# Reordering the opening of a GFNet-plus-FFN kernel: all x at once, five weight buffers, weight conversions in other places

## The chip, the cores and the metric

The kernel runs on one core of a Trainium2 chip. The metric is device time in microseconds (us) of one execution; with one core there is no slowest core to choose.

Engines are named as in the profile: PE is TensorE's matmuls, PEld its weight loads, DVE is VectorE, ACT is ScalarE, POOL is GpSimd, SP is SyncE. L312 is line 312 of the kernel in question; the changed kernel's lines differ by one or so from those of the kernel before, past the first helpers.

## The reference

```python
batch, seq, dim = (8, 3008, 256);  n_tokens, d_model, d_ff = (24064, 256, 2048)

def _attn_ref(x, filt_r, filt_i):
    X = np.fft.rfft(x, axis=1)
    F = (filt_r + 1j * filt_i)[None, :, :]
    return np.fft.irfft(X * F, n=x.shape[1], axis=1).astype(np.float32)

def _moe_ref(x, w_in, w_out):
    h = x @ w_in
    g = np.where(h > 0.0, h, np.exp(np.minimum(h, 0.0)) - 1.0)
    return (g @ w_out).astype(np.float32)
# out = _moe_ref(_attn_ref(x, filt_r, filt_i).reshape(B * S, D), w_in, w_out)
```

A filter along the sequence is followed by a two-layer network of width 2048 over all tokens. The weights arrive as 64-bit numbers and are turned into 32-bit ones on the core.

## The kernel before

The Fourier transform of length 3008 is done as two factors (47 and 64), with an intermediate z written to HBM and read back in another order. The second factor multiplies by the filter and goes part of the way back; its result goes through HBM again (yd) and is read per block of tokens. Then comes the token loop: 8 batches of 6 blocks, four *quads* each, a quad being one quarter of the hidden width for one block, some 13.6 us long. From batch 1 on, the transform of the next batch is hidden in the token loop. For batch 0 there is nothing to hide it behind: that is the opening, and the change is only about it.

```python
def x_load(b, c, queue=nc.sync):                  # one of six chunks of x, 4 buffers
    t = xs[b, c] = xp.tile([P, XC, D], FP32, tag="xc", name="xc")
    ...
    w = tas[b, c] = tap.tile([P, XC, P], FP32, tag="ta", name="ta")
    queue.dma_start(w, ta_d[:, ts(c, XC), :])
    ...

def a_unit(b, c):                                 # first factor, one chunk
    t = t1s[b, c] = t1p.tile([P, XC, D], FP32, tag="t1", name="t1")
    for r in (0, 2):
        ...matmuls into psa
        nc.scalar.activation(out=t[:, r:r + 2, :], in_=ps, func=AXT.Copy)

def b_unit(b, g, f=None):                         # second factor, one of eight units
    ...matmuls of t (a read of z) into psr ("re"), psi ("im")
    nc.vector.tensor_tensor(out=sr, in0=re, in1=f[:, 0], op=ALU.mult)
    nc.vector.tensor_tensor(out=si, in0=re, in1=f[:, 1], op=ALU.mult)
    nc.vector.tensor_tensor(out=p, in0=im, in1=f[:, 1], op=ALU.mult)
    nc.vector.tensor_tensor(out=q, in0=im, in1=f[:, 0], op=ALU.mult)
    nc.gpsimd.tensor_tensor(out=sr, in0=sr, in1=p, op=ALU.subtract)
    nc.gpsimd.tensor_tensor(out=si, in0=si, in1=q, op=ALU.add)

def bi_unit(b, g):                                # the way back
    ...matmuls into pa ("pva"), pb ("pvb")
    nc.scalar.activation(out=t[:, 0:2, :], in_=pa, func=AXT.Copy)
    nc.scalar.activation(out=t[:, 2:4, :], in_=pb, func=AXT.Copy)

def w_convert(k):                                 # piece k of 16, 512 KB of 64-bit numbers
    nc.vector.tensor_scalar(out=m, in0=hi, ...)                        # wm, the mask
    nc.scalar.activation(out=l, in_=lo, func=AXT.Identity, ...)        # wl
    nc.scalar.activation(out=f, in_=m, func=AXT.Identity, ...)         # wf: waits for wm
    ...four operations on e, one on f, one product, all on VectorE
    if j % 2 == 1:                                                     # odd pieces only
        ...four VectorE sums of the seven-product scheme
```

Pieces 4q and 4q+1 belong to the first layer's quarter q, 4q+2 and 4q+3 to the second layer's. In the traces of this case VectorE and ScalarE run their instructions in the program's order (below, a ScalarE copy that stands behind conversion 10 starts only at 121.10, behind that conversion's step at 120.08), so the place of a `w_convert` sets what stands behind it on both. The order of the opening before:

```python
for k in range(2):
    w_fetch(k)                                    # GpSimd's queue, 3 buffers
for c in range(XBUFS):                            # 4
    x_load(0, c, nc.scalar)
...
w_fetch(2)
f_read_first(ff)                                  # the filter, 3.1 MB, GpSimd's queue
for c in range(NXC):                              # 6
    a_unit(0, c)
    if c + XBUFS < NXC:
        x_load(0, c + XBUFS, nc.scalar)
    z_write(0, c)
    w_convert(c)
    w_fetch(3 + c)
z_read(0, 0)
z_read(0, 1)
for g in range(NG + 2):                           # 8 units, bi_unit two behind b_unit
    ...bi_unit(0, g - 2), b_unit(0, g, ff[:, g]), z_read(0, g + 2), y_write(0, g - 2)
    if g % 2 == 1:
        k = 6 + g // 2
        w_convert(k)
        w_fetch(k + 3)
...
y_read(0, 0)
w_convert(11)
w_fetch(14)
...
n_unit(0, 0)                                      # first matmuls on tokens ("psn")
x_load(1, 0)
...
for k in range(12, 16):                           # behind quads 0, 0, 1, 2
    at((0, 0, 1, 2)[k - 12], 1, w_convert, k)
```

## Time and profile before

| | before |
|---|---|
| time, 3 runs | 2762.31 us median (2762.2 to 2765.57) |
| span of the profiled run, granted clock | 2761.7 us, 0.980 |
| first VectorE multiplication of the second factor ("S") | 74.79 us |
| first matmul on tokens | 131.14 us |
| first matmul of quad 1 | 153.31 us |

The prediction below shows the page and the stages. More lines of the timeline; columns are start, length, engine, line, operation, output<-inputs, and in brackets the idle time of the engine ahead of it and what ended it:

```profile
120.30 0.59 ACT L239 ACTIVATE t<-pvb 128x512 f32<-128x512 f32 x1
...
131.14 3.75 PE L266 MATMUL psn<-tn,t 128*128 128x128 f32 x16 [11.41 <-DMA t<-yd]
...
133.79 0.39 DVE L288 TENSOR_TENSOR ys<-y 128x224 f32<-128x224 f32 x1 [2.10 <-ACT y L268]
```

The last copy of the second factor ends at 120.89, the array starts on tokens when the read of yd has landed, and the first VectorE operation on tokens waits for ScalarE's copy, so VectorE has time to spare there. The second factor itself, from S to the start of conversion 9, in the view by stretch (stretch, length, busy time of PE, PEld, DVE, ACT, POOL, granted clock, DMA share, GB/s):

```profile
74.79:115.49 40.70, 28.10 (x115) 8.92 (x108) 36.53 (x58) 9.78 (x18) 21.12 (x20) 0.63 0.57 156
```

and the waits of its VectorE for the array, over the 44 us from 0.8 us behind S (instruction, releaser, us in total, times, longest):

```profile
DVE sr L223 <- PE psi L211: 3.2, 2, 2.1
```

VectorE is busy 36.53 of 40.70 us there and waits only 3.2 us for the array.

### The profile page before, as it was taken

The numbers are of one execution on the slowest core, as the hardware profiler recorded it, in microseconds if no ns is written. First come the engines' busy times: TensorE is split into PE (matmuls) and PEld (weight loads), VectorE is DVE, ScalarE is ACT, GpSimd is POOL, SyncE is SP. The second block draws the span as 40 slices with busy tenths as digits, with TensorE's granted clock in tenths as the row PEclk, the third lists the DMA queues.
The fourth block names the chain that finished last, engine by engine and source line by source line (L and its number), as shares of the span: only waits on it lengthen the run. The fifth ranks groups of instructions, "written<-read, shape, count | busy, mean of one in ns | idle before, by whom it ended". The sixth has DMA issues, their size and how long they took to land.

```text
span 2761.7 us, 36465 instructions
## 1 busy us (share of the span) xinstructions
PE 2661.4 (96%) x13376; PEld 2281.0 (83%) x13376; DVE 2021.7 (73%) x3428; ACT 1331.3 (48%) x2281; POOL 268.4 (10%) x322
## 2 busy tenths in 40 slices
PE   2689999999999999999999999999999999999998
PEld 1288778987899878998789877898789987899887
DVE  4777877777776777767776787767877677777776
ACT  2254455544455444554455544454454544454544
POOL 3311210002000120001200021000210012000000
PEclk7599999999999999999999999999999999999999
DMA  9654421433114331242313332143321223110100
GB/s 227 174 136 119 106 56 30 115 90 99 43 47 117 76 91 37 70 115 71 79 50 87 87 88 68 37 106 94 97 61 39 72 69 94 37 39 19 25 22 16
DMA packets 141634, 214.51 MB, mean 78 GB/s; under 512 B 25268, under 2 KB 99142, under 8 KB 141456
## 3 DMA queue, kind: packets, MB, share of 16 engines
q1 hardware_dynamic: 122656, 173.60, 24.7%
q0 software_dynamic: 17792, 36.93, 5.4%
q8 instruction: 106, 1.74, 0.3%
q10 hardware_dynamic: 1008, 1.64, 0.2%
q14 instruction: 72, 0.59, 0.1%
HBM read 137.04 MB, written 78.12 MB: 78 GB/s over the span
## 4 chain that ended last, share of the span: by engine, by line
PE 86%; DVE 7%; ACT 3%; DMA 2%; issue 2%; POOL 0%; SPq 0%; DVEq 0%; ACTq 0%; POOLq 0%
PE po L385 37%; PE pha L312 11%; PE phc L312 11%; PE phd L312 11%; PE phb L312 5%; PE psa L167 3%; PE psn L266 2%; PE pva L211 2%; PE psr L211 2%; PE pso L424 2%; DVE g L317 1%; ACT e L323 1%; ACT e L324 1%; DVE c L403 1%; DVE g L328 1%
## 5 line engine op out<-in xcount | busy, mean ns | idle before, releaser
L385 PE MATMUL po<-g,wo 128*128 128x256 f32 (+1 forms) x5376 | 1324.2, 375 | 0.0
L385 PEld LDWEIGHTS po<-g,wo 128*128 128x128 f32 x5376 | 1021.5, 190 | 116.2
L323 ACT ACTIVATE e<-g 128x512 f32<-128x512 f32 (+1 forms) x576 | 357.6, 621 | 599.5 <-DVE g L317 599.3
L324 ACT ACTIVATE e<-e 128x512 f32<-128x512 f32 (+1 forms) x768 | 477.6, 622 | 24.4
L312 PE MATMUL pha<-y,wi 128*128 128x256 f32 (+1 forms) x1536 | 396.3, 380 | 8.7 <-ACT g L332 8.6
L317 DVE TENSOR_TENSOR g<-phc,g 128x512 f32<-128x512 f32 (+1 forms) x384 | 259.5, 676 | 194.9 <-PE phc L312 194.8
L328 DVE SCALAR_TENSOR_TENSOR g<-e,g 128x512 f32<-128x512 f32 (+1 forms) x576 | 387.4, 673 | 11.6 <-ACT e L324 11.1
L323 ACT ACTIVATE e<-pha 128x512 f32<-128x512 f32 (+1 forms) x192 | 113.0, 588 | 531.1 <-PE pha L312 531.1
L312 PEld LDWEIGHTS pha<-y,wi 128*128 128x128 f32 x1536 | 285.2, 190 | 93.1 <-ACT t L238 34.1
L317 DVE TENSOR_TENSOR g<-phd,g 128x512 f32<-128x512 f32 (+1 forms) x384 | 261.0, 680 | 87.0 <-PE phd L312 66.0
L328 DVE SCALAR_TENSOR_TENSOR g<-e,pha 128x512 f32<-128x512 f32 (+1 forms) x192 | 129.4, 674 | 257.8 <-ACT e L324 257.8
L227 POOL TENSOR_TENSOR sr<-sr,sp 128x512 f32<-128x512 f32 x64 | 81.1, 1268 | 1304.4 <-DVE sp L225 1304.4
L312 PE MATMUL phc<-ys,wi 128*128 128x256 f32 (+1 forms) x768 | 195.5, 377 | 2.6 <-DVE si L224 2.6
L312 PE MATMUL phd<-y,wi 128*128 128x256 f32 (+1 forms) x768 | 195.4, 377 | 1.3
L312 PE MATMUL phb<-ys,wi 128*128 128x256 f32 (+1 forms) x768 | 193.8, 375 | 0.4 <-DVE ys L290 0.4
L312 PE MATMUL phc<-y,wi 128*128 128x256 f32 (+1 forms) x768 | 194.0, 375 | 0.0
L312 PE MATMUL phd<-ys,wi 128*128 128x256 f32 (+1 forms) x768 | 193.7, 375 | 0.0
L312 PEld LDWEIGHTS phc<-ys,wi 128*128 128x128 f32 x768 | 145.3, 191 | 23.7 <-issue 7.8
L312 PEld LDWEIGHTS phd<-y,wi 128*128 128x128 f32 x768 | 145.3, 191 | 22.5 <-PE phc L312 6.5
L332 ACT ACTIVATE g<-pha 128x512 f32<-128x512 f32 (+1 forms) x192 | 112.7, 587 | 105.3 <-PE pha L312 105.1
L312 PEld LDWEIGHTS phb<-ys,wi 128*128 128x128 f32 x768 | 145.8, 190 | 17.2 <-PE pha L312 0.7
L312 PEld LDWEIGHTS phd<-ys,wi 128*128 128x128 f32 x768 | 145.8, 190 | 16.5
(98 smaller groups left out, 2781.1 us busy)
## 6 DMA issues: line engine op xcount, KB each, us to landing
z<-t SPq DMA_DIRECT2D x192, 128.0 KB, 3.8
t<-z SPq DMA_DIRECT2D x128, 192.0 KB, 3.7
yd<-t SPq DMA_DIRECT2D x128, 192.0 KB, 2.8
t<-yd SPq DMA_DIRECT2D x192, 128.0 KB, 4.1
xc<-in_x_dram SPq DMA_DIRECT2D x88, 256.0 KB, 4.6
out_dram<-o SPq DMA_DIRECT2D x176, 128.0 KB, 2.4
f<-fd POOLq DMA_DIRECT2D x112, 192.0 KB, 3.6
tn<-tn_t SPq DMA_DIRECT2D x48, 256.0 KB, 4.2
```

What stands on the lines that cost most here:

```text
L167: nc.tensor.matmul(ps[:, u, :], w[:, r + u, :], xt[:, r + u, :], start=True, stop=True)
L211: nc.tensor.matmul(ps[:, u:u + w, :], table[k, v, :], rhs[k, u:u + w, :], start=True, stop=True)
L227: nc.gpsimd.tensor_tensor(out=sr, in0=sr, in1=p, op=ALU.subtract)
L266: nc.tensor.matmul(ps[:, ts(q, P)], t[:, i - 4 * m, ds(dh * P, P)], w[:, i - 4 * m, :], start=True, stop=True)
L312: nc.tensor.matmul(banks[key][:, a, 0:h], w_in[q][:, COMBO[n], a, :], y[n], start=start and a == 0, stop=True, skip_group_check=True)
L317: nc.vector.tensor_tensor(out=g[o], in0=i0, in1=i1, op=ALU.add)
L323: nc.scalar.activation(out=e, in_=src, func=AXT.Relu, scale=-1.0)
L324: nc.scalar.activation(out=e, in_=e, func=AXT.Exp, scale=-1.0)
L328: nc.vector.scalar_tensor_tensor(out=g[n], in0=es[n], scalar=1.0, in1=src, op0=ALU.subtract, op1=ALU.max)
L332: nc.scalar.activation(out=g["t1"], in_=mm(1, "a", True), func=AXT.Copy)
L385: nc.tensor.matmul(po[i][:, u, 0:h], w_out[q][:, COMBO[n], a, :], g[n][:, a, :], start=q == 0 and a == 0 and n in (1, 3, 6, 4), stop=True, ...
L424: nc.tensor.transpose(ps[0:w, u, ts(dh, P)], c[dh][:, ds((2 * a + u) * P, w)], eye)
```

## The change

The intent: let the first factor go at the pace of x, with nothing of the weights ahead of its copies; keep the transfers full by loading weights further ahead; take the next batch's x out of the stretch in which the first tokens' data are read back; and take the last weight pieces out of it too. `wait_x(c)` and the copy into `junk` below are one-element copies on GpSimd that wait until a load has landed, and so hold back the loads that stand behind them in GpSimd's order. Besides, the filter is read in two halves and its buffer is cleared on GpSimd instead of VectorE.

```diff
-            zs[b] = zp.tile([96, K2, D], FP32, tag="z", name="z")
+            zs[b] = zp.tile([96, K2 + 1, D], FP32, tag="z", name="z")
 ...
-        wd = wds[k] = fbufs[k % FBUFS]...
+        wd = wds[k] = wbufs[k % 5 if k < 12 else (2, 0, 1, 2)[k - 12]]...
 ...
+        CONVERTS = {1: 6, 3: 7, 5: 8, 7: 9, 8: 10, 9: 11}
+            wbufs += [... "wb%d" ... for i in range(2)]
+            more = [(... "xb%d", ... "tb%d") for i in range(NXC - XBUFS)]
             for k in range(2):
                 w_fetch(k)
-            for c in range(XBUFS):
-                x_load(0, c, nc.scalar)
-            nc.vector.memset(ff, 0.0)
+            for c in range(NXC):
+                x_load(0, c, nc.scalar, more[c - XBUFS] if c >= XBUFS else None)
+            nc.gpsimd.memset(ff, 0.0)
 ...
+            w_convert(0)
+            w_convert(1)
+            wait_x(3)
             w_fetch(2)
-            f_read_first(ff)
+            w_fetch(3)
+            wait_x(5)
+            for a in range(2):
+                f_read_first(ff, a)
+            for k in range(4, 7):
+                w_fetch(k)
             for c in range(NXC):
                 a_unit(0, c)
-                if c + XBUFS < NXC:
-                    x_load(0, c + XBUFS, nc.scalar)
                 z_write(0, c)
-                w_convert(c)
-                w_fetch(3 + c)
+            for k in range(2, 6):
+                w_convert(k)
+                w_fetch(k + 5)
 ...
-                if g % 2 == 1:
-                    k = 6 + g // 2
-                    w_convert(k)
-                    w_fetch(k + 3)
+                if g in CONVERTS:
+                    w_convert(CONVERTS[g])
+                if g == 1:
+                    w_fetch(11)
+                if g == 4:
+                    w_fetch(12)
+                if g in (5, 6):
+                    x_load(1, g - 5)
 ...
-        w_convert(11)
-        w_fetch(14)
+        w_convert(12)
+        nc.gpsimd.tensor_copy(out=junk[0:1], in_=t4s[0, 0][0:1, 0, 0:1])   # the read has landed
+        for k in (13, 14, 15):
+            w_fetch(k)
         n_unit(0, 0)
-        x_load(1, 0)
 ...
-        for k in range(12, 16):
-            at((0, 0, 1, 2)[k - 12], 1, w_convert, k)
+        for k in (13, 14, 15):
+            at(max(k - 14, 0), 1, w_convert, k)
```

More of the change, by code (lines that the diff above doesn't have):

```diff
@@ L145, in raw, with x_load @@
         return bass.AP(tensor=src.tensor, offset=src.offset + row * D, ap=ap)
-    def x_load(b, c, queue=nc.sync):
-        t = xs[b, c] = xp.tile([P, XC, D], FP32, tag="xc", name="xc")
+    def x_load(b, c, queue=nc.sync, place=None):
+        t, w = place or (xp.tile([P, XC, D], FP32, tag="xc", name="xc"), tap.tile([P, XC, P], FP32, tag="ta", name="ta"))
+        xs[b, c], tas[b, c] = t, w
         skip = 1 if c == 0 else 0
@@ L153, in x_load @@
             nc.gpsimd.memset(t[64:P, 0, :], 0.0)
-        w = tas[b, c] = tap.tile([P, XC, P], FP32, tag="ta", name="ta")
         queue.dma_start(w, ta_d[:, ts(c, XC), :])
@@ L178, in z_write @@
             r0 = p * H + c * XC
-            nc.sync.dma_start(zs[b][r0:r0 + XC, :, :].rearrange("n k d -> k n d"), t[p * 32:p * 32 + 32, :, :])
+            nc.sync.dma_start(zs[b][r0:r0 + XC, 0:K2, :].rearrange("n k d -> k n d"), t[p * 32:p * 32 + 32, :, :])
     def z_read(b, g):
@@ L189, in f_read, with f_read_first @@
             nc.gpsimd.dma_start(t[r].rearrange("p c u d -> p (c u d)"), fd[g, a].rearrange("q c u d -> q (c u d)"))
-    def f_read_first(t):
+    def f_read_first(t, a):
+        r = a * 64
         for c, src in enumerate((filt_r, filt_i)):
-            for a in range(2):
-                r = a * 64
-                nc.gpsimd.dma_start(t[r:r + 24, :, c, :, :].rearrange("q g u d -> q g (u d)"),
-                                    raw(src, 2 * a, [[64 * D, 24], [4 * D, NG], [1, 2 * D]]))
-                for u in range(2):
-                    g0 = 1 if a == u == 0 else 0
-                    for r0, n in ((24, 16), (40, 7)):
-                        nc.gpsimd.dma_start(t[r + r0:r + r0 + n, g0:NG, c, u, :],
-                                            raw(src, 64 * (r0 - 23) - 4 * g0 - 2 * a - u,
-                                                [[64 * D, n], [-4 * D, NG - g0], [1, D]]))
-            nc.gpsimd.dma_start(t[24:48, 0, c, 0, :], raw(src, 32, [[64 * D, 24], [1, D]]))
+            nc.gpsimd.dma_start(t[r:r + 24, :, c, :, :].rearrange("q g u d -> q g (u d)"),
+                                raw(src, 2 * a, [[64 * D, 24], [4 * D, NG], [1, 2 * D]]))
+            for u in range(2):
+                g0 = 1 if a == u == 0 else 0
+                for r0, n in ((24, 16), (40, 7)):
+                    nc.gpsimd.dma_start(t[r + r0:r + r0 + n, g0:NG, c, u, :],
+                                        raw(src, 64 * (r0 - 23) - 4 * g0 - 2 * a - u,
+                                            [[64 * D, n], [-4 * D, NG - g0], [1, D]]))
+            if a == 0:
+                nc.gpsimd.dma_start(t[24:48, 0, c, 0, :], raw(src, 32, [[64 * D, 24], [1, D]]))
     def tile_mm(ps, table, k, rhs, special):
@@ L440 @@
     wds = {}
+    wbufs = list(fbufs)
     def w_fetch(k):
         q, j = divmod(k, 4)
-        wd = wds[k] = fbufs[k % FBUFS].bitcast(U32).rearrange("p c u d -> p (c u d)").rearrange("p (a w) -> p a w", w=2)
+        wd = wds[k] = wbufs[k % 5 if k < 12 else (2, 0, 1, 2)[k - 12]].bitcast(U32).rearrange("p c u d -> p (c u d)").rearrange("p (a w) -> p a w", w=2)
         if j < 2:
@@ L513, with wait_x @@
     with tc.manual_schedule():
+        CONVERTS = {1: 6, 3: 7, 5: 8, 7: 9, 8: 10, 9: 11}
         with tc.tile_pool(name="boot", bufs=1) as bp:
             ff = bp.tile([P, NG, 2, 2, D], FP32, name="ff")
+            wbufs += [bp.tile([P, 2, 2, D], FP32, name="wb%d" % i) for i in range(2)]
+            more = [(bp.tile([P, XC, D], FP32, name="xb%d" % i), bp.tile([P, XC, P], FP32, name="tb%d" % i))
+                    for i in range(NXC - XBUFS)]
+            def wait_x(c):
+                nc.gpsimd.tensor_copy(out=junk[0:1], in_=xs[0, c][0:1, 0, 0:1])
             for k in range(2):
                 w_fetch(k)
-            for c in range(XBUFS):
-                x_load(0, c, nc.scalar)
-            nc.vector.memset(ff, 0.0)
-            nc.gpsimd.tensor_copy(out=junk[0:1], in_=xs[0, 2][0:1, 0, 0:1])
+            for c in range(NXC):
+                x_load(0, c, nc.scalar, more[c - XBUFS] if c >= XBUFS else None)
+            nc.gpsimd.memset(ff, 0.0)
             for t, d in ((gb, gb_d), (gr, gr_d), (gi, gi_d)):
                 nc.gpsimd.dma_start(t, d)
+            w_convert(0)
+            w_convert(1)
+            wait_x(3)
             w_fetch(2)
-            f_read_first(ff)
+            w_fetch(3)
[4 more added lines that the diff above has]
+                w_fetch(k)
             for c in range(NXC):
                 a_unit(0, c)
-                if c + XBUFS < NXC:
-                    x_load(0, c + XBUFS, nc.scalar)
                 z_write(0, c)
-                w_convert(c)
-                w_fetch(3 + c)
+            for k in range(2, 6):
+                w_convert(k)
+                w_fetch(k + 5)
             z_read(0, 0)
@@ L567, in at @@
             plan.setdefault((quad, place), []).append((fn, a))
-        for c in range(1, XBUFS):
-            at(c - 1, 0, x_load, 1, c)
-        for k in range(12, 16):
-            at((0, 0, 1, 2)[k - 12], 1, w_convert, k)
-        at(0, 1, w_fetch, 15)
+        for c in range(2, XBUFS):
+            at(c - 2, 0, x_load, 1, c)
+        for k in (13, 14, 15):
+            at(max(k - 14, 0), 1, w_convert, k)
         at(3, 1, f_arrange)
```

## The prediction

> **What bounds the kernel now.** I began with the page: share of busy time, then the row of slices.
>
> ```profile
> PE 2661.4 (96%) x13376; PEld 2281.0 (83%) x13376; DVE 2021.7 (73%) x3428; ACT 1331.3 (48%) x2281; POOL 268.4 (10%) x322
> ...
> PE   2689999999999999999999999999999999999998
> ...
> PEclk7599999999999999999999999999999999999999
> DMA  9654421433114331242313332143321223110100
> ```
>
> TensorE is busy except in the first two slices (69 us each), and these are also the only ones with a low granted clock and the ones with the busiest DMA. Next I asked for busy time by stretch. From 300 to 2700 us TensorE works 2396.10 of 2400 us, so nothing there is to be had from waits; the change leaves that part's instructions alone. Everything is decided before quad 1 of the token loop (a quad is one quarter of the hidden width for one block of tokens) settles at about 153 us:
>
> ```profile
> 0.00:30.00 30.00, 12.43 (x40) 8.48 (x40) 17.80 (x24) 8.00 (x13) 9.64 (x21) 0.99 1.00 241
> 30.00:75.00 45.00, 7.91 (x25) 4.78 (x28) 15.53 (x33) 7.48 (x13) 12.97 (x23) 0.50 0.88 208
> 75.00:121.00 46.00, 32.12 (x123) 9.57 (x116) 41.66 (x64) 12.58 (x24) 23.88 (x22) 0.61 0.54 146
> 121.00:131.00 10.00, 0.00 (x0) 0.00 (x0) 9.55 (x21) 2.38 (x4) 1.91 (x4) 0.50 0.89 265
> 131.00:153.00 22.00, 14.59 (x68) 13.36 (x68) 14.46 (x30) 9.65 (x18) 1.24 (x2) 0.81 1.01 245
> ```
>
> The columns are the stretch, its length, busy time of PE, PEld, DVE, ACT, POOL, clock, DMA share, GB/s. Four stages follow. First factor, 0 to 75: DMA is full and no engine is. Second factor, 75 to 121: VectorE is busy 41.66 of 46 us. Then 10 us in which TensorE waits for the result through HBM. Then the first quad and a hole. The chain of waits, in order of time, says which transfers the first stage hangs on:
>
> ```profile
> 4.40 11.32 DMA xc<-in_x_dram
> ...
> 20.04 13.04 DMA ff<-in_filt_r_dram
> 33.90 11.16 DMA ff<-in_filt_i_dram
> ...
> 47.58 6.99 DMA f<-in_moe_w_out_dram
> ...
> 63.43 4.87 DMA z<-t
> 68.36 4.28 DMA t<-z
> ```
>
> First x, then the filter, then a weight piece queued behind it, then the conversion of that piece on ScalarE and VectorE, and only behind it in ScalarE's order the copies of the last two x chunks, whose write to z comes last. The timeline gives the start of the second factor, and the hole of the last stage:
>
> ```profile
> 74.79 0.69 DVE L223 TENSOR_TENSOR sr<-psr,ff 128x512 f32<-128x512 f32 x1 [5.65 <-PE psi L211]
> ...
> 122.60 0.42 DVE L470 TENSOR_SCALAR wm<-f 128x512 uint32<-128x512 uint32 x1
> ...
> 153.31 1.86 PE L312 MATMUL pha<-y,wi 128*128 128x224 f32 x4 [7.05 <-ACT g L332]
> ```
>
> **What the Trainium skill says.** "DMA: Bandwidth & Descriptors", section "Issuing engines are not separate DMA queues": transfers of all issuing engines run on the same 16 DMA engines and interleave. The trace agrees: between 30 and 40 us the SyncE queue took 59.1% and the GpSimd queue 46.8%, together only 201 GB/s. So reordering moves waits, but does not make bytes cheaper. The same page, section "Latency and other measured facts", tells of loss at large power-of-two HBM row pitches, smallest 512 KiB; here z goes from a 32 KiB pitch to 33 KiB, which that table does not reach. "SBUF — State Buffer", section "Who interferes with whom": a VectorE tensor_scalar that enters a two-port mode and a GpSimd operation exclude each other. The trace agrees: L474 takes 0.42 us alone, 1.49 us beside GpSimd's 1.45 us addition. "TensorE: Matmul & The Clock Gate", section "What's actually happening": after an idle window the array runs at half clock. The trace agrees: after the 7.05 us hole four matmuls took 1.86 us instead of 0.92.
>
> **Part by part.** I call S the first VectorE multiplication of the second factor (74.79 before) and reckon the rest from it.
>
> *First stage.* Removed: the wait of x chunk 5 for a buffer (landed at 41), and the ScalarE copies standing behind conversions that wait for weights. So z no longer hangs on weights and should be complete near 50 instead of 68. But conversions 2 to 5 now all stand in VectorE's order after the x copies and ahead of the first multiplication, and pieces 4 and 5 are queued behind the filter. So S hangs on piece 5. Bytes until then: x 3.1 MB, its tables 1.6, z 3.1, filter 3.1, six pieces of 0.52 = 3.1, second-factor tables 0.2, two reads of z 0.8: 15.0 MB. At before's rates, 241 GB/s to 30 us (7.2 MB) and 218 GB/s from 30 to 68 (the DMA view of that stretch), the other 7.8 MB take 36 us: piece 5 at 66. With fewer stalls of the queues, as between 60 and 70 (234 GB/s), 63. Behind it: a conversion without sums took VectorE 3.7 us in before (122.60 to 126.25), one with its four sums 5.5 (54.66 to 60.12); conversions 4 and 5 in a row, from piece 4's landing some 2 us earlier (0.52 MB at 234 GB/s), end 5.5 to 7 us behind piece 5. S = 68.5 to 73, I take **70: 4.8 us won**. Pieces 6 and 7, which before moved in this stage, move later.
>
> *Second factor.* Eight units with four multiplications of 0.6 us each and a conversion after every second stay as they were, with VectorE as the limit. But the new place of conversions (after units 1, 3, 5, 7, then two in the tail) puts conversion 10 ahead of the last unit's two ScalarE copies. In before these copies ran at 119.81 to 120.90. Now they follow ScalarE's second step of conversion 10, which waits for VectorE's mask, at 122.60 in before, because conversion 9 with its sums is ahead. Mask 0.42, ScalarE 0.63, copies 1.1: end at 124.8 in before's time. **3.9 us lost.**
>
> *Through HBM.* Before, from the last copy to the first matmul was 131.14 less 120.90 = 10.2 us: 3.8 for the write, 1.3 issue, 5.0 for the last read, beside weights and the next x at 265 GB/s. x now goes during the second factor, where DMA was 54% busy, and weights 13 to 15 wait until the read has landed. A read of this kind takes 2.4 us when alone (80 to 125 us); so write 3.0, issue 1.3, read 3.0: 7.3. **2.9 won.** But VectorE now has conversions 9 to 12 in a row, 7.1 + 3.7 + 5.4 + 3.7 = 19.9 us from 115.47, to 135.4 in before's time; the tokens' first subtraction, 133.79 before, stands behind: it comes at +1.6. So of 3.9 - 2.9 = +1.0, +1.5 remains.
>
> *First quads.* The hole stays: two conversions still stand after quad 0, ahead of the copy L332 of quad 1. They were 12 and 13 (sums last), now 13 and 14: 13's four sums stand before 14's mask, so the copy comes 4 x 0.43 = 1.7 us later: **+1.7**. Conversion 15 moves one quad earlier and leaves the quad after it: TensorE lost 1.6 us there between 181 and 195; I count -0.5.
>
> Sum: -4.8 + 1.5 + 1.7 - 0.5 = -2.1 us. I go somewhat lower, to **2757**, because the bytes' rate is the softest term and a queue that never stalls, or the padded z, would raise it: 15.0 MB at 260 GB/s would give piece 5 at 60 and S at 65.
>
> **Rivals.** (1) *z is the bound and weights are not*: if S followed z (50 + read 4.5 + units' matmuls 2) S would be 58 and the time 2748. For it: in before VectorE waited 5.65 us for the psi matmuls, behind z. Against: the order of instructions puts conversion 5 first. (2) *The filter's transfers bound*: in before it took from 18.6 to about 53 us to issue and land. Now it starts once the last x has landed, about 30; the same 34 us would make it 64, and pieces 4 and 5 land at 67 to 69; S = 74, nothing won, and +2.7 from the rest: 2765. (3) *Padding z does much*: all reads and writes of z faster. In the loop that would be hidden (TensorE 99.8% busy); in the opening worth perhaps 3 us. (4) *A fuller second factor*: x of 1.5 MB among the reads of z could delay a unit; DMA is half idle there, so I give it at most 1 us.
>
> **Range and chances.** The first stage can lie from 0 to 14 us better, the rest +1 to +5 worse: 2748 to 2764 for eight in ten. Two per cent is 55 us, over a third of the whole opening, so same is nearly certain.
>
> **What the new profile would show.** z complete near 50 and its reads waiting no more for ScalarE; the first L223-like multiplication at 68 to 72, released by a conversion rather than by matmuls; the last pair of copies of the second factor behind a conversion's ScalarE step; last read of yd in about 3 us; and a hole of 8 to 9 us before quad 1. Wrong it would be if the multiplication started before 64 or after 75, if the hole were gone, or if the loop after 300 us had changed its pace.

## The result, and the profile after

| | before | after |
|---|---|---|
| time, 4 runs each of the same rounds | 2763.66 us (2762.2 to 2765.57) | 2762.14 us (2761.47 to 2763.48) |
| span of the profiled run | 2761.7 us | 2761.7 us |
| ratio | | 0.9995, 95% interval 0.9977 to 1.0012 |

Ratios, here and below, are the mean time of one kernel's runs over that of the other's of the same rounds, so not quite the ratio of the medians quoted. The change does nothing that can be measured, and the prediction's range and class hold; its point was 5 us too low. The profile says that a lot moved nonetheless, though not in the slices of the page, where the row of granted clocks still shows two low slices:

```profile
PEclk7599999999999999999999999999999999999999
```

The stages after, in the view by stretch:

```profile
0.00:30.00 30.00, 14.78 (x43) 10.06 (x44) 11.84 (x22) 8.34 (x13) 16.96 (x24) 1.00 1.00 267
30.00:69.00 39.00, 6.49 (x19) 3.15 (x18) 16.11 (x34) 7.72 (x13) 13.93 (x25) 0.54 1.06 224
69.00:122.00 53.00, 37.25 (x124) 9.77 (x122) 46.16 (x74) 13.61 (x25) 22.70 (x20) 0.53 0.60 162
122.00:130.00 8.00, 0.27 (x1) 0.30 (x2) 7.66 (x17) 2.60 (x4) 2.05 (x4) 0.50 0.82 217
130.00:154.00 24.00, 15.12 (x69) 13.57 (x68) 18.17 (x36) 9.89 (x18) 1.06 (x2) 0.78 0.70 199
```

Against the stretches of before: the first stage is 6 us shorter, at 267 and 224 GB/s instead of 241 and 208. The second is 7 us *longer* (53 instead of 46). The wait for the first tokens' data is 2 us shorter, and the first quad with its hole (the idle time of TensorE ahead of quad 1) 2 us longer (24 instead of 22), with VectorE busy 18.17 us there instead of 14.46.

The chain of waits of the first stage after, in order of time (start, length, what):

```profile
13.37 7.94 DMA xc<-in_x_dram
21.33 7.04 DMA z<-t
28.38 14.76 DMA z<-t
...
45.69 13.17 DMA z<-t
58.91 7.77 DMA t<-z
...
66.82 0.65 PE psi L211
```

The filter and the weights have left this chain. What took their place is z itself: three writes of it took 7.0, 14.8 and 13.2 us, and the last part of the read that the first unit needs was issued only at 58.91. The timeline shows that the other chain ends at the same moment:

```profile
59.83 0.43 DVE L471 TENSOR_SCALAR wm<-wb 128x512 uint32<-128x512 uint32 x1 [7.61 <-DMA wb<-in_moe_w_in_dram]
...
68.51 0.42 DVE L494 TENSOR_TENSOR wi<-wi 128x256 f32<-128x256 f32 x1
68.89 0.69 DVE L223 TENSOR_TENSOR sr<-psr,ff 128x512 f32<-128x512 f32 x1
```

Piece 4 lands at 59.83, conversions 4 and 5 run back to back for 9.06 us, and the first multiplication follows at 68.89 without a gap. The array's psi for it is done at about 68.8, too.

Now the end of the second factor and the start of the tokens:

```profile
119.63 0.42 DVE L471 TENSOR_SCALAR wm<-f 128x512 uint32<-128x512 uint32 x1
120.08 0.63 ACT L473 ACTIVATE wf<-wm 128x512 f32<-128x512 uint32 x1 [2.10 <-DVE wm L471]
121.10 0.59 ACT L239 ACTIVATE t<-pvb 128x512 f32<-128x512 f32 x1
...
129.73 3.75 PE L266 MATMUL psn<-tn,t 128*128 128x128 f32 x16 [12.97 <-ACT wf L473]
131.79 0.69 DVE L487 TENSOR_TENSOR wi<-wf,we 128x512 f32<-128x512 f32 x1
132.45 0.39 DVE L288 TENSOR_TENSOR ys<-y 128x224 f32<-128x224 f32 x1
...
153.90 1.86 PE L312 MATMUL pha<-y,wi 128*128 128x224 f32 x4 [8.77 <-ACT g L332]
```

The last copies stand behind conversion 10's `wf`, as the diff says. The releaser named at 129.73 is an inference of the profile; in the program these matmuls need only the read of yd and a ScalarE copy that ended long before, so it was the read; experiments 6 and 8, whose program is the same there, start at 129.72 and 129.76 with the read as releaser. The first operation on tokens, L288, now starts as the last one of conversion 12 ends, with no gap: here VectorE has become the limit. And the hole ahead of quad 1 grew from 7.05 to 8.77 us.

Inside the second factor, the same 40.70 us from S, and the waits:

```profile
68.89:109.59 40.70, 31.66 (x108) 8.85 (x106) 34.70 (x54) 9.72 (x18) 19.60 (x18) 0.54 0.69 188
```

```profile
DVE sr L223 <- PE psi L211: 6.0, 4, 2.1
```

Over the 44 us from 0.8 us behind S, VectorE waits 6.0 us for the array instead of 3.2, and the granted clock is 0.54 instead of 0.63.

The whole account, in us from the span's start; "first stage alone" is an experiment told below:

| milestone | before | after | gained or lost on the way | first stage alone |
|---|---|---|---|---|
| S, first multiplication | 74.79 | 68.89 | -5.9 | 69.00 |
| conversion 9 starts | 115.47 | 112.49 | +2.9 | 111.94 |
| last copy of the second factor ends | 120.89 | 121.69 | +3.8 | 117.37 |
| first matmul on tokens | 131.14 | 129.73 | -2.2 | 124.94 |
| first VectorE operation on tokens, L288 | 133.79 | 132.45 | +0.1 | 128.09 |
| quad 1's first matmul | 153.31 | 153.90 | +1.9 | 147.06 |
| second block's first matmul | 313.60 | 313.23 | -1.0 | 307.05 |

The steps sum to -0.4; the spans of the two profiled runs are equal. From 300 to 2700 us TensorE is busy 2396.10 and 2395.76 of 2400 us: nothing happens there.

### The profile page after: what moved, and what is told of

It is laid out like the page before. It is cut to its first block, busy times and chain, and to the rows that moved or that the text cites. A ratio compares the mean times of both kernels' runs of the same rounds, so it can differ in the third digit from the quotient of the medians.

```text
span 2761.7 us, 36475 instructions
## 1 busy us (share of the span) xinstructions
PE 2667.8 (97%) x13376; PEld 2281.5 (83%) x13376; DVE 2017.9 (73%) x3427; ACT 1332.3 (48%) x2281; POOL 275.3 (10%) x325
## 4 chain that ended last, share of the span: by engine, by line
PE 86%; DVE 7%; ACT 3%; DMA 2%; issue 2%; ACTq 0%; DVEq 0%; POOL 0%; SPq 0%
PE po L385 37%; PE pha L312 11%; PE phc L312 11%; PE phd L312 11%; PE phb L312 5%; PE psa L167 3%; PE psn L266 2%; PE psr L211 2%; PE pva L211 2%; PE pso L424 2%; DMA z<-t 1%; DVE g L317 1%; ACT e L323 1%; ACT e L324 1%; DVE c L403 1%
```

## The experiments

Theory: the first stage's gain of 6 us is real and is eaten by where the change puts its conversions (conversion 10 ahead of the last copies, a row of four conversions on VectorE, two conversions ahead of quad 1), and by a slower second factor. Rivals: the gain is lost whatever follows, because a later wait absorbs it; the padded z or a buffer holds the first stage; the early x costs or gains on its own. Twelve kernels were run. All outputs are right. All had class "same" at the 2% level; what separates them are a few microseconds, so the intervals matter. A single profile can lie some 1 or 2 us off its kernel's median (the profiled run of the changed kernel took 2763.48, the slowest of its four).

### 1. z without the padding

```diff
-            zs[b] = zp.tile([96, K2 + 1, D], FP32, tag="z", name="z")
+            zs[b] = zp.tile([96, K2, D], FP32, tag="z", name="z")
```

> The changed kernel with z back at a row pitch of 32 KiB; nothing else undone. Theory: the pitch hardly matters, because the stage is bound by bytes; the first multiplication of the second factor stays at 68.9 us within 1 us, and the time within 0.1% of the changed kernel's 2762. Rival (the padding raised the rate to the 314 GB/s seen between 20 and 30 us): that rate falls towards before's 253 GB/s, the last piece of z lands 3 us or more later than 58.9, and the multiplication comes at 71 or later.

Measured: 2762.52, ratio to before 0.9993 (0.998 to 1.0005). S is 69.13, the last read of z is issued at 58.68. The padding does nothing that this run could see.

### 2. One conversion per quad

Conversions 13, 14, 15 behind quads 0, 1, 2 instead of 0, 0, 1:

```diff
-            at(max(k - 14, 0), 1, w_convert, k)
+            at(k - 13, 1, w_convert, k)
```

> The changed kernel with conversions 13, 14 and 15 behind quads 0, 1 and 2, one each, instead of two behind quad 0. Theory: TensorE's hole before quad 1 is made by the second conversion standing ahead of ScalarE's copy L332, so the hole falls from 8.8 to about 3.5 us, quad 1 starts near 148.6, of which up to 1 us is lost again behind quad 2: 4 to 5 us less, 2757 to 2758. Rival (VectorE's work is conserved, so a conversion costs the same wherever it stands): the hole shrinks, but quads 1 and 2 lose as much, and the time stays within 1 us.

Measured: 2757.40 (2755.63 to 2759.1), ratio 0.9975 (0.9963 to 0.9988). The timeline:

```profile
146.49 1.86 PE L312 MATMUL pha<-y,wi 128*128 128x224 f32 x4 [3.40 <-ACT g L332]
```

The hole shrinks from 8.77 to 3.40 us, and the later quads lose 2.0 us in all (0.38, 1.19 and 0.42) where they lost 1.5 in the changed kernel. The time falls by about 5 us against the changed kernel. So the second of two conversions between one quad and the next costs about 5 us. This is not a loss that the change brought in: the kernel before had two there as well, with a hole of 7.05 us, and the change's own share is the 1.7 us by which the hole grew.

### 3. The last copies ahead of conversion 10

```diff
-        CONVERTS = {1: 6, 3: 7, 5: 8, 7: 9, 8: 10, 9: 11}
+        CONVERTS = {1: (6,), 3: (7,), 5: (8,), 7: (9,), 9: (10, 11)}
```

> The changed kernel with conversion 10 moved behind the last unit's two ScalarE copies of the second factor. Theory: the copies end 3.9 us earlier (117 instead of 121.7) and the first token matmul moves forward by 2 to 4 us, but the tokens' first subtraction on VectorE stays at 132.5 within 0.7 us, because conversions 9 to 12 in a row are ahead of it; the time stays within 1 us. Rival (the copies are what the path hangs on): the subtraction and the time go down by 3 to 4 us.

Measured: 2761.69, ratio 0.999 (0.9978 to 1.0003). The timeline of this run:

```profile
116.81 0.59 ACT L239 ACTIVATE t<-pvb 128x512 f32<-128x512 f32 x1
125.66 3.75 PE L266 MATMUL psn<-tn,t 128*128 128x128 f32 x16 [9.43 <-DMA t<-yd]
131.77 0.38 DVE L288 TENSOR_TENSOR ys<-y 128x224 f32<-128x224 f32 x1
```

The copies end 4.3 us earlier and the array starts on tokens 4.1 us earlier, but L288 only 0.7 us earlier (S itself was 0.4 earlier). Four conversions in a row on VectorE, 9 to 12, set the start of the tokens. The delay of the copies is real, and hidden.

### 4. The same, and only conversions 9 to 11 ahead of the tokens

As experiment 3, with conversions 12, 13, 14, 15 behind quads 0, 1, 2, 3, and piece 15 fetched behind quad 0 (not shown in the cut):

```diff
-        w_convert(12)
 ...
-        for k in (13, 14, 15):
-            at(max(k - 14, 0), 1, w_convert, k)
+        for k in (12, 13, 14, 15):
+            at(k - 12, 1, w_convert, k)
```

> Conversion 10 behind the copies as in the run before, and conversions 12 to 15 one behind each of quads 0 to 3. Theory: with conversion 12 gone from VectorE's row the first subtraction comes at about 128.7 instead of 132.5, the hole before quad 1 is about 3.5 us, and quads 2 to 4 lose about 3 us together to the conversions now there: 6 us less, 2756. Rival (work conserved): quads 1 to 4 lose all of it, and the time stays within 2 us of the changed kernel.

Measured: 2764.95 (2762.63 to 2766.53), ratio 1.0003 (0.9989 to 1.0017): a miss. The front is as expected: L288 at 128.70, a hole of 3.4 us, quad 1 at 143.72, ten microseconds ahead of the changed kernel. But the TensorE waits have a new entry:

```profile
PE po L385 <- DVE wo L487: 7.2, 1, 7.2
```

Conversion 15 belongs to the second layer's last quarter. Behind quad 3 it stands immediately ahead of its first use, and TensorE waits 7.2 us for it. With the other waits of these quads, the ten microseconds have shrunk to 0.8 by the second block's first matmul (312.41). Conversion 15 can stand behind quad 2, as in experiment 2, and not behind quad 3.

### 5. Before, with the next batch's x early

The kernel before, with `x_load(1, 0)` and `x_load(1, 1)` at units 5 and 6 of the second factor:

```diff
+                if g in (5, 6):
+                    x_load(1, g - 5)
 ...
-        x_load(1, 0)
```

> The kernel before with one part of the change alone: the next batch's first two x chunks are loaded within the second factor. Theory: the read of the second factor's result no longer shares DMA with x, the first token matmul moves from 131.1 to about 128.5, but the tokens' first subtraction only from 133.8 to about 131.8, where conversion 11 ends on VectorE: 2 us less than before. Rival (the x loads take as much from the second factor as they free later): its last copies end later than 120.9 and the time stays within 1 us or rises.

Measured: 2764.49 against 2763.55, ratio 0.9999 (0.9985 to 1.0013): a miss. The second factor is not slower (conversion 9 at S + 40.7, as in before), but the first token matmul comes at 133.31, 12.0 us behind the last copy, not sooner. Taking x out of that stretch does not, by itself, shorten the read. Experiment 7 shows the reverse: there the next x is loaded behind the read just as in before, and the read is short.

### 6. Six buffers for the first factor's results

The ScalarE copies of chunks 3 to 5 write to the used x tiles, so that no copy waits for a write of z to finish:

```diff
-                a_unit(0, c)
+                a_unit(0, c, x0[c - 3] if c >= 3 else None)
```

> The changed kernel with six places instead of three for ScalarE's copies of the first factor (the copies of chunks 3 to 5 go to the x tiles that are used up). Theory: the three waits of 5.7 to 6.9 us of ScalarE for z writes vanish, z lands some 4 us earlier (about 55), but the first multiplication stays at 68.9 within 0.7 us, since conversions 4 and 5, whose weights come behind the filter, are ahead of it on VectorE; time unchanged within 1 us. Rival (z sets the start): the multiplication comes about 3 us or more earlier.

Measured: 2762.16, ratio 0.9992 (0.998 to 1.0005). S is 69.48; the last read of z is issued at 59.25, no earlier than the 58.91 of the changed kernel. In the chain of waits these copies do wait for writes of z; taking that wait away changes nothing, so the buffers are not what holds z.

### 7. The first stage alone

The changed kernel's first stage, with the tail of the kernel before: conversions 6 to 10 behind units 1, 3, 5, 7 and at the end, 11 behind the read, 12 and 13 behind quad 0, then 14 and 15; the next x, and pieces 14 and 15, fetched where they were in before.

```diff
-        CONVERTS = {1: 6, 3: 7, 5: 8, 7: 9, 8: 10, 9: 11}
+        CONVERTS = {1: 6, 3: 7, 5: 8, 7: 9, 9: 10}
 ...
-        w_convert(12)
+        w_convert(11)
 ...
-        for k in (13, 14, 15):
-            at(max(k - 14, 0), 1, w_convert, k)
+        for k in range(12, 16):
+            at((0, 0, 1, 2)[k - 12], 1, w_convert, k)
```

> The changed kernel's first stage (x at once, five weight buffers, filter behind x, conversions 2 to 5 together) with everything from the second factor on as before: conversion 10 behind the last copies, 11 while the result is read, 12 and 13 behind quad 0, the next x behind the read. Theory: the first multiplication comes at 68.9, the last copies end at 115, the first token matmul is at 125.3 and quad 1 starts at 147.4: the whole 5.9 us reach the end, 2757.5. Rival (weights 6 to 8 pushed out of the first stage delay the second factor by as much): the last copies end at 118 or later and the time is within 2 us of before.

Measured: 2756.17 (2756.08 to 2757.31), ratio 0.9972 (0.9958 to 0.9986), 7.4 us below the median of before.

```profile
69.00 0.68 DVE L223 TENSOR_TENSOR sr<-psr,ff 128x512 f32<-128x512 f32 x1
...
124.94 3.70 PE L266 MATMUL psn<-tn,t 128*128 128x128 f32 x16 [8.73 <-DMA t<-yd]
...
147.06 1.86 PE L312 MATMUL pha<-y,wi 128*128 128x224 f32 x4 [7.05 <-ACT g L332]
```

S is as early as in the changed kernel, and quad 1 is 6.25 us earlier than in before, with the old hole of 7.05. So the rival that a later wait absorbs the gain is out: it reaches the end when the change's own tail is left away. Part of it is lost on the way here too (the last copy ends at S + 48.4, not S + 46.1, although no x is loaded early), and 2.7 us come back because the way from the last copy to the first token matmul takes 7.6 instead of 10.2 us.

### 8. Pieces 4 and 5 ahead of the filter

As experiment 6, with `w_fetch(4)` and `w_fetch(5)` in front of `f_read_first`.

```diff
             wait_x(5)
+            w_fetch(4)
+            w_fetch(5)
             for a in range(2):
                 f_read_first(ff, a)
-            for k in range(4, 7):
-                w_fetch(k)
+            w_fetch(6)
```

> The six places of the other run, and weight pieces 4 and 5 fetched ahead of the filter instead of behind it: the same bytes, another order. Theory: what the first multiplication waits for is the last of the transfers that it needs; now that is the filter itself (about 62.5 to 64) without 9 us of conversions behind it, so it comes at 63 to 66 instead of 68.9 and the time falls by 3 to 5 us from the changed kernel's 2762. Rival (the stage is bound by bytes alone, in whatever order): 68 or later, time unchanged.

Measured: 2762.73, ratio 0.9996 (0.9983 to 1.0008): the rival's result. S does not move, only its releaser:

```profile
68.99 0.69 DVE L223 TENSOR_TENSOR sr<-psr,ff 128x512 f32<-128x512 f32 x1 [22.74 <-PE psi L211]
```

VectorE is now done with the conversions 22.74 us ahead of S, and waits for the array, which waits for z (last read issued at 60.79). Together with experiment 6: with the same bytes on the way, which transfers come first only decided which of them came last. The reading that the bytes ahead of S are what counts follows from this only by argument; experiment 9 tries it.

### 9. Fewer bytes ahead of S

As experiment 7, with pieces 4 and 5 ahead of the filter, and pieces 6 to 10 held back until the second read of z has landed:

```diff
+            for k in range(4, 6):
+                w_fetch(k)
             for a in range(2):
                 f_read_first(ff, a)
-            for k in range(4, 7):
-                w_fetch(k)
 ...
+            nc.gpsimd.tensor_copy(out=junk[64:65], in_=t2s[0, 1][64:65, 0, 0:1])
+            w_fetch(6)
+            w_fetch(7)
```

(8 and 9 are fetched at unit 0, 10 at unit 1, instead of behind conversions 3 to 5.)

> The kernel of the first stage alone (new first stage, tail as before), with weight pieces 4 and 5 ahead of the filter and pieces 6 to 10 held back until z has been read. Theory (the first multiplication waits for bytes, and pieces 6 to 8, not needed yet, share DMA with the last of z and its reads): some 1 to 1.5 MB less before it, at about 235 GB/s 4 to 6 us; the multiplication comes at 63 to 65 instead of 68.5, and the time at 2751 to 2753. Rival (the last of z is bound by its own latency, not by sharing): the multiplication stays at 68 or later, 2756.

Measured: 2755.61 (2754.53 to 2755.8), ratio 0.9973 (0.9959 to 0.9986). S moves to 66.39, 2.6 us ahead of experiment 7, with 15.02 MB moved until then instead of 16.79. This agrees with bytes being the limit, but experiment 11 puts the scatter of S in this form at 3 to 4 us, and the time gains nothing that could be told from experiment 7 (ratios 0.9973 and 0.9972). Conversion 6 now waits for its piece. In the lines below the releaser of the first is the one-element copy that waits for the same data of z:

```profile
66.39 0.69 DVE L223 TENSOR_TENSOR sr<-psr,ff 128x512 f32<-128x512 f32 x1 [2.75 <-POOL junk L552]
...
73.34 1.94 DVE L471 TENSOR_SCALAR wm<-f 128x512 uint32<-128x512 uint32 x1 [1.19 <-DMA f<-in_moe_w_out_dram]
```

The last copy ends only 0.8 us earlier than in experiment 7. The bytes held back are missed a few microseconds later.

### 10. Holding back alone

As experiment 7, with pieces 6 to 10 held as in experiment 9, and pieces 4 and 5 left behind the filter (the diff is that of experiment 9 without its first two added lines, and with a range of 4 and 5 in place of the two removed).

> As the run above, but pieces 4 and 5 behind the filter as in the changed kernel. Theory: z and its reads come earlier as above, but pieces 4 and 5 land where they did and 9 us of conversions follow, so the multiplication stays at 68 to 69 and the time at 2756, that of the first stage alone. Rival (conversions 4 and 5 never set the start): it comes as early as in the run above.

Measured: 2758.45 (2758.23 to 2758.61), ratio 0.9984 (0.9972 to 0.9997): 2 us worse than experiment 7. S stays at 69.56 because conversions 4 and 5 still set it, and the held pieces are late; the last copy ends at 119.26. Holding back pays nothing unless what waits ahead of S goes first.

### 11. The best parts together

Experiment 9, with conversion 12 ahead of the tokens as in the change, and 13, 14, 15 one per quad as in experiment 2:

```diff
+        w_convert(12)
+        w_fetch(15)
 ...
-        for k in range(12, 16):
-            at((0, 0, 1, 2)[k - 12], 1, w_convert, k)
+        for k in range(13, 16):
+            at(k - 13, 1, w_convert, k)
```

> As the first run here, with conversion 12 while the result is read and 13, 14, 15 one behind each of quads 0 to 2. Theory: the hole before quad 1 falls from 7.05 to 3.4 us, but the tokens' first subtraction is 3.7 us later because conversion 12 now stands ahead of it; the time stays within 1.5 us of the first run here. Rival (a conversion behind a quad costs more than one in the tail): 3 us less.

Measured: 2754.87 (2753.5 to 2757.05), ratio 0.9972 (0.996 to 0.9985), the lowest median, but not to be told from experiment 9's 2755.61, nor, by its ratio, from experiment 7 (0.9972 for both). The hole falls from 6.98 us in experiment 9 to 3.40, yet the time hardly moves: reckoned from S, L288 comes at 64.57 instead of 60.92 us, because conversion 12 now stands ahead of it. These 3.65 us take back the 3.58 of the hole, as the expectation said. S was 62.74 in this profile, although up to there the program is that of experiment 9 (66.39). Each has only one profile, and this one fell on the fastest of its runs, so 3 or 4 us of S are scatter in this form of the opening. S is still the earliest in these two profiles, the only ones with pieces 4 and 5 first and the others held. In the changed kernel and experiments 1, 2, 3, 6 and 7, where pieces 4 and 5 come behind the filter, S lies within 68.3 and 69.5.

### 12. Before, with x early and the second block's read later

Experiment 5, with the second block's read of yd moved out of the stretch, to quad 0:

```diff
-                    at(t + s - (1 if m == 0 else 2), 0, y_read, b, m)
+                    at(0 if (b, m) == (0, 1) else t + s - (1 if m == 0 else 2), 0, y_read, b, m)
```

> The kernel before with the next x early, as in the run that gained nothing (last read of the second factor's result landed at 133.3 instead of 131.1), and the second block's read moved from directly behind the first to one quad later. Theory: the second block's read and table, 0.77 MB, took the place of x beside the first read; with it gone the first token matmul comes at 130 or earlier and the time is 1 to 2 us below before. Rival (the weight pieces fetched at the same time, not the second read, hold the first read up): it stays at 131 or later and the time at before's.

Measured: 2763.48 against 2763.59, ratio 1.0001 (0.9988 to 1.0015): a miss. The first token matmul comes at 131.51, 11.4 us behind the last copy. In place of the second block's read, the third x chunk moved up in SyncE's queue. What does go with the length of this read over five kernels is what the GpSimd queue, the weights, moved between the last copy and the first token matmul:

| kernel | GpSimd queue, MB | last copy to first token matmul, us |
|---|---|---|
| after | 0.00 | 8.0 |
| first stage alone (7) | 0.19 | 7.6 |
| before | 1.05 | 10.2 |
| before, x early, read later (12) | 1.12 | 11.4 |
| before, x early (5) | 1.22 | 12.0 |

The other nine runs, all with the new first stage, moved 0.00 to 0.16 MB and took 7.2 to 8.3 us. Experiment 7 comes closest to a test: SyncE issues the read, and then the next x, in the same order and spacing as in before (the x table 1.75 us behind the first read in both), and only the weights are fewer. But its first stage differs too, and no run changed the weights alone in that stretch. So x is out as the cause, and the weights are argued and not shown.

## Why the prediction was right, and where it was not

**The first stage, "S = 68.5 to 73, I take 70".** Right in size: 68.89, so 5.9 us won where 4.8 were foretold. The prediction counted 15.0 MB by 63 to 66 us; the trace moved 14.94 MB in its first 62 us (241 GB/s), though not quite the bytes counted, since pieces 6 and 7 were under way before the reads of z had landed. The mechanism was half right. Conversions 4 and 5 do end at S, but "z should be complete near 50" failed: its last read was issued at 58.91. The prediction took z off the weights' wait and forgot that z shares the same full DMA engines. Experiments 6 and 8 show that neither buffers nor order alone move S.

**The second factor, "stay as they were, with VectorE as the limit".** This failed, at +2.9 us. VectorE waits for the array twice as long, and the granted clock is lower. That the clock is the cause is not shown: experiment 5, too, had a low clock (0.58) over these 40.7 us and lost nothing, and experiment 2, at 0.50, lost 2.2 us where the changed kernel lost 2.9 at 0.54. That the early x is not the cause is shown: experiment 5 has it and is not slower, experiment 7 lacks it and is slower by 2.3. The same two runs speak against fuller transfers as such: over the 40.7 us they moved 191 GB/s in experiment 5 and 164 in experiment 7. The cause stays open; every run with the new first stage has the slower second factor (42.9 to 44.8 us from S to conversion 9, against 40.7 in the three runs without it).

**The last copies, "3.9 us lost".** Right: 3.8. But experiment 3 shows that this delay is not on the path: without it the tokens' VectorE work starts only 0.7 us earlier.

**Through HBM, "2.9 won".** Measured 2.2. Of the two reasons given, x beside the read fell in experiments 5, 7 and 12; the weights held back fit, by correlation only. The 2.4 us that the prediction calls a read "alone" is the first of four reads, issued at 124.71 beside weights and x at 253 GB/s; so it was not alone. In the changed kernel the transfers to and from yd took 2.6 to 4.7 us there.

**VectorE's row of four conversions, "+1.5 remains".** Right. From S to L288 it is 63.56 instead of 59.00 us, so +4.6; less the 2.9 of the slower second factor, +1.7. L288 begins where conversion 12 ends.

**The hole, "+1.7", and "-0.5" later.** The hole grew by 1.72 us, and the later quads gave back 1.0. Experiment 2 adds what the prediction did not ask: having two conversions there costs about 5 us in the changed kernel, so much more than the order of the two.

**The sum and the step to the point.** The terms summed to -2.1; measured was -0.4 up to the second block, 0.0 over the profiled span and -1.5 between the medians. That the sum came so near is partly luck: the 2.9 us of the second factor were not foreseen, and a first stage 1.1 us better than foretold and other small terms covered some of them. The further 3 us from there to 2757 "because the bytes' rate is the softest term" were the worst step: they pushed from one side only. The rate did come out a little above the prediction's sum (241 GB/s to 62 us, where 15.0 MB by 63 to 66 us is 227 to 238), and S came 1.1 us earlier than foretold, not 5. Without this step, and with the 2.9 us, the sum would have been +0.8. The range's upper end, 2764, also leaves out a case of its own terms (nothing won and 5 us lost is 2767); the measured time lies 1.9 us inside.

**The rivals.** z as the bound (1): half true, its chain ends at the same time as the weights', but its last needed read was issued at 58.91 and not near 50. The filter as the bound (2): out, piece 4 landed behind it at 59.83 and not at 67. The padding (3): nothing, experiment 1. A fuller second factor (4): it was slower, by more than the 1 us allowed, but not because of x.

## What to carry to other kernels

A stretch saved on the path is only worth what the next in-order row lets through: follow it to every engine that has its own work waiting. Here six microseconds were won in the first stage; by the start of the tokens VectorE's row, with a slower second factor and one conversion more, had taken back 4.6 of them, and the longer hole and what stands beside it took 1.9. Put background work once per period, behind what the path needs next and well ahead of its own first use; two at once made a hole, and one directly ahead of its use made a wait of 7.2 us. In this first stage, with its transfers full (share 1.00 and more), changing their order or adding buffers changed the last wait's name and not its end.

## What the Trainium skill lacked or had wrong

- "DMA: Bandwidth & Descriptors", section "Latency and other measured facts": its table of HBM row pitches begins at 512 KiB. Here 32 KiB against 33 KiB made no difference (S 69.13 and 68.89, time 2762.52 and 2762.14 us), so a line for small pitches could say that padding them is not needed, as far as this goes.
- The same page, section "Anatomy of one DMA — SWDGE (gpsimd) path": its fit, 2.0 us plus bytes over 436 GB/s, gives 2.3 us for 128 KB. With all queues full, the filter's 128 KB pieces on GpSimd's queue took 7.6 to 9.8 us from issue to landing (medians, from 30 us on, both kernels). The page gives no landing time of a whole transfer beside full queues. (These pieces are rows of 1 KB, and the fit was not tried here on an idle queue, so how much of the difference is the load and how much the shape is open.)
- "TensorE: Matmul & The Clock Gate", section "What's actually happening": it says after what idle and what busy time the clock changes, not how much idle a busy window may hold. In the second factor the array was busy 27 to 33 of 40.7 us and the granted clock was between 0.50 and 0.63 for the same instructions. What decides between them no run here shows.
- No page that I found tells what a background task costs by its place in two engines' orders at once. Here a conversion cost nothing visible ahead of the last copies (experiment 3: 0.4 us in time), about 5 us as the second of two between quads (experiment 2), and a wait of 7.2 us directly ahead of its use (experiment 4).
